# Two pieces of side work joined into one with two strands, late weights awaited one by one, and corrected durations in a planner

## The chip, the cores and the metric

The kernel runs on one core of a Trainium2 chip. The core has a matrix engine (PE, with its weight load shown apart as PEld), a vector engine (DVE), an activation engine (ACT), GpSimd (POOL), and SyncE (SP), which here issues nearly all DMA transfers. The metric is the device time of one execution in microseconds. The kernel before took 860.47, 861.98 and 862.07 us in three runs, a median of 861.98 us. The execution that the profiler recorded took 859.36 us, of which its span is 857.6 us.

## The reference, cut to what matters

One transformer block over 2048 tokens of width 512 in bfloat16: attention with 32 heads of size 16, then a gated feed-forward part (hidden width 1792), each behind a layer norm whose scale and shift come from a small vector `c`.

```python
sa, ca, ga, sb, cb, gb = split(silu(c) @ w_mod)
h = layernorm(x) * (1 + ca) + sa
q, k, v = split_heads(h @ wqkv)                      # 32 heads of 16
x = x + ga * (softmax(q @ k.T / 4) @ v) @ wo
h = layernorm(x) * (1 + cb) + sb
x = x + gb * (gelu(h @ w_gate) * (h @ w_up)) @ w_down
```

The scores are 32 x 2048 x 2048 numbers, and each of them needs an exponential.

## The kernel before

The tokens are cut into six sets (`SETS`): three of 512 queries (sets 0, 1, 2), one of 256 (set 3) and two of 128 (sets 4, 5). Each set is gone through in eight units `qd` of four heads. A unit consists of rounds; a round is four tiles of scores of 128 x 512, one for each head. All in all there are 2048 tiles, and a place in this order is called a position; `ends[k]` is the position at which set k's scores are finished (`ends[2]` = 1536, `ends[3]` = 1792, `ends[4]` = 1984, the last is 2048).

**The main line of work.** PE computes two or three tiles of scores into PSUM (`ps_sc`), ACT turns them into exponentials `E` (line 327, one instruction for 1024 or 1536 columns), and PE multiplies them with the values into `ps_pv` (line 314). For some rounds, which I call vector rounds, DVE takes the place of ACT: four instructions of 512 columns each (`dreg<-ps_sc` or `mreg<-ps_sc`, line 339) make an approximate exponential, and four more of 2048 columns (`mreg<-dreg`, `mreg<-mreg`) make shifted copies. PE then multiplies five versions instead of one with the values. A vector round takes four tiles off ACT and puts eight instructions on DVE. While one is being filled, each group has two tiles for ACT and one for DVE.

**The side work.** Everything else runs as generators that hand PE one matmul at a time, in the order of a list made by `plan`: the projections of the first layer, and for each finished set k the output projection `side_wo(k)` (needs the normalized attention outputs `onorm` of all eight units), the second layer norm as a chain of small DVE tasks, and `side_ffn(k)`: transposes, then gate products `G` and up products `U` for 14 blocks of 128 hidden columns, then the down projection. All side matmuls go through one PSUM bank, `ps_mi`. Only the first generator of the list is asked; while it waits for something (`until`), no side work is done at all.

**Who sets the order.** The instruction streams are written out by a planner when the kernel is built. It goes through the work with its own model of durations (`model` and `cost`) and always issues what it believes can start next. Each entry of `plan` has a first position and a due position; the columns that remain, divided by the positions up to the due one, earn credit. Side work advances when there is credit. From `ends[2]` on, a vector round is begun only while the credit is under 2048 (of at most 4096) or while side work waits for `onorm` or `osb`. In other words, side work behind its schedule keeps vector rounds from being begun.

**The late weights.** For sets 0 to 2 the feed-forward weights are streamed from memory into staging buffers. For sets 3 to 5 they stay in SBUF: ten parts of 256 KB are loaded early, and eleven late ones (seven of `w_up`, one of `w_gate`, three of `w_down`) go into places that the down projection of set 2 uses to its end. They are issued one per two positions after `("ffn", 2)` is done, and `side_ffn(3)` begins with a wait for `"weights"`, which is set after the last of them has been issued. After that, `scale_down` multiplies the down weights by `gb` on DVE.

**Set 3's second layer norm** writes into `tb2`, the front of `hreg`; the products `prodT` that set 2's down projection reads lie in the same place.

At the end, `near_end` computes the last normalizations of set 4 on PE, `side_wo(4)` follows, then the first part of set 4's feed-forward work; the tail finishes sets 4 and 5 after the last exponential.

Of the kernel before, what the change touches and what calls it, by code (L numbers as in the profile page):

```python
# [13 lines left out]
P = 128  # L14
# [65 lines left out]
class _Recorder:  # L80
# [166 lines left out]
    def model(self, op, t, cost):  # L247
# [6 lines left out]
        elif eng == "pe":  # L254
# [3 lines left out]
            if mode != self.pe_mode:  # L258
                t = max(t, self.pe_end + 105)
# [6 lines left out]
            end = t + max(cols, 64) / 2.4  # L266
# [20 lines left out]
    def cost(self, eng, out, ins, kind):  # L287
        n = 1
        for _, k in (out if kind != "bn" else ins[0]).ap[1:]:
            n *= int(k)  # L290
        aps = [out] + list(ins)
        ps = any(self.kind.get(a.tensor.name) == "ps" for a in aps)
        small = all(mybir.dt.size(a.dtype) == 2 for a in aps)
        if eng == "act":
            return n * 0.833 + (57 if ps else 92)
        if eng == "pool":
            return n * 3.0 + 100
        f = 1
        if not ps:
            f = {("ts", True): 4, ("ts", False): 2, ("tt", True): 2}.get((kind, small), 1)  # L300
        elif small:
            f = 1.4
        return n * 1.042 / f + 68
# [116 lines left out]
class _Kernel(_Recorder):  # L420
# [12 lines left out]
    def alloc(self):  # L433
# [9 lines left out]
        self.tb2 = hreg[:, 0:4 * D].rearrange("p (t n) -> p t n", t=4)  # L443
        wreg = sb("wreg", [P, NDC * 1536], BF16)
# [407 lines left out]
    def weight_parts(self):  # L852
# [9 lines left out]
        return g[:6] + d[:4], u + g[6:] + d[4:]  # L862
# [23 lines left out]
    def normed(self, k, i):  # L886
        return self.E[:, NSL - 1, :] if k == len(SETS) - 1 else self.tb2[:, i, :]
# [75 lines left out]

    def side_wo(self, gi):
# [4 lines left out]
        for i in range(n):  # L969
            for g in self.merged(gi):  # L970
# [11 lines left out]
    def side_ffn(self, gi, part=None):  # L982
# [28 lines left out]
        else:  # L1011
            yield from self.until("weights")
# [14 lines left out]
        def G(ci):  # L1027
# [3 lines left out]
            load(0, ci + 1)  # L1031
            for b0 in range(0, m, kpb):
# [10 lines left out]
        def U(ci):  # L1043
# [4 lines left out]
            load(1, ci + 1)  # L1048
            for b0 in range(0, m, kpb):
# [28 lines left out]
        if part is not None:  # L1078
# [4 lines left out]
            return  # L1083
        if not flow:
# [59 lines left out]
    def plan(self, ends, nsplit):  # L1144
# [15 lines left out]
        due = (ends[1] + 30, ends[2] + 30, ends[3] + 30, ends[4] - 20)  # L1160
        for k, e in enumerate(due):
            s0 = ends[k] + 33
            w.append((lambda k=k: self.side_wo(k), s0, min(e, s0 + 15 * SETS[k][1] // P)))
            w.append((lambda k=k: self.side_ffn(k), s0, e))
        k, s0 = len(SETS) - 2, ends[-2] - 16
        w.append((lambda: self.near_end(k, 6, self.mi[:, 0:P]), s0, s0))
        w.append((lambda: self.near_end(k, 7, self.mi[:, 0:P]), s0, s0))
        w.append((lambda: self.side_wo(k), s0, s0))
# [49 lines left out]
    def stream(self):  # L1218
# [140 lines left out]
        while cg <= group[units[-1]]:  # L1359
            parts = early or late  # L1360
            if parts and pos >= loaded and (pos >= ends[2] + 8 if early else ("ffn", 2) in self.have):
                parts.pop(0)()
# [426 lines left out]
```

## Time and profile before

| what | us |
|---|---|
| three runs | 860.47, 861.98, 862.07 |
| the profiled execution, its span | 859.36, 857.6 |
| ACT busy in the span | 830.9 (97%) |
| PE busy | 788.0 (92%) |
| DVE busy | 705.6 (82%) |
| exponentials on ACT | 698 instructions, 803.2 |
| last exponential of the main line ends | 836.1 |

Busy time is a sum over stages. Up to 836 us ACT works on exponentials nearly without a gap; from there to the end a chain over all engines finishes the last 256 tokens. The attention outputs of set 3's eight units leave PSUM between 625.05 and 722.44 us and are normalized (`onorm<-osb,rb`) between 642.35 and 736.92 us; sets 4 and 5 follow. The granted PE clock was full in all slices but the first and the last moments.

### The profile page before, as it was taken

To read this page: it belongs to the slowest core of one execution; us is meant where nothing else is said; L and a number is where in the kernel's file an instruction comes from. 1 tells how busy PE (TensorE), PEld (TensorE's weight loads), DVE (VectorE), ACT (ScalarE), POOL (GpSimd) and SP (SyncE) were. 2 spreads that over 40 slices of the span, in tenths; PEclk is the share of its full clock that TensorE was granted. 3 is DMA by queue.
4 is the path that set the end of the run, shared out by engine and by line. 5 is a ranking of instruction groups with operands and counts; after the bars stand their busy time and mean duration, and the time that the engine had idled before them with its cause. 6 is when DMAs were issued, how large, how long until landed. Compare 5 with 4: busy or idle time off the path is not lost.

```text
span 857.6 us, 27732 instructions
## 1 busy us (share of the span) xinstructions
PE 788.0 (92%) x12443; PEld 285.8 (33%) x12445; DVE 705.6 (82%) x1363; ACT 830.9 (97%) x747; POOL 4.5 (1%) x12
## 2 busy tenths in 40 slices
PE   8899998999999998999999899999998999988987
PEld 3333332322222222222222222222343333435556
DVE  7855989787999898999899999988887877477664
ACT  7999999999999999999999999999999999999992
POOL 1000000000000000000000000000000000000000
PEclk9999999999999999999999999999999999999999
DMA  9000000000002112110003102110233222150000
GB/s 313 27 15 17 5 10 11 10 13 9 8 9 78 47 37 57 55 37 21 12 18 91 49 21 60 37 55 12 59 97 116 57 70 56 33 144 11 20 7 14
DMA packets 66169, 38.97 MB, mean 45 GB/s; under 512 B 18657, under 2 KB 63906, under 8 KB 66050
## 3 DMA queue, kind: packets, MB, share of 16 engines
q1 hardware_dynamic: 65520, 36.67, 15.3%
q8 instruction: 97, 1.59, 0.8%
q10 hardware_dynamic: 530, 0.53, 0.2%
q14 instruction: 22, 0.18, 0.1%
HBM read 33.81 MB, written 2.61 MB: 42 GB/s over the span
## 4 chain that ended last, share of the span: by engine, by line
ACT 72%; PE 13%; DVE 8%; DMA 4%; SPq 2%; issue 1%; DVEq 0%
ACT E L327 69%; PE ps_mi L314 6%; PE ps_sc L314 5%; PE ps_pv L314 2%; ACT wreg L327 2%; DMA rb<-scr_rec 2%; SPq L377 2%; DVE st L367 1%; DVE mreg L339 1%; DMA den<-scr_den 1%; DMA scr_rec<-rden 1%; DVE dreg L339 1%; DVE wreg L344 1%; DVE hreg L339 1%; DVE nwt L331 0%
## 5 line engine op out<-in xcount | busy, mean ns | idle before, releaser
L327 ACT ACTIVATE E<-ps_sc 128x1536 bf16<-128x1536 f32 (+2 forms) x698 | 803.2, 1344 | 13.7 <-PE ps_sc L314 13.1
L314 PE MATMUL ps_sc<-qT,kmo 32*128 32x512 bf16 (+2 forms) x1408 | 182.7, 323 | 10.8 <-ACT E L327 8.7
L314 PE MATMUL ps_sc<-qT,kme 32*128 32x512 bf16 (+2 forms) x1408 | 176.1, 323 | 15.7 <-ACT E L327 13.0
L314 PE MATMUL ps_pv<-E,vaug 128*17 128x512 bf16 (+2 forms) x2396 | 171.3, 319 | 4.7 <-DVE osb L348 2.3
L339 DVE TENSOR_SCALAR dreg<-ps_sc 128x512 uint16<-128x512 f32 x200 | 137.7, 690 | 36.5 <-PE ps_sc L314 33.6
L339 DVE TENSOR_SCALAR mreg<-dreg 128x2048 uint16<-128x2048 uint16 x200 | 131.5, 682 | 1.7 <-PE ps_pv L314 1.5
L314 PE MATMUL ps_mi<-wreg,mreg 128*32 128x512 bf16 (+2 forms) x1504 | 110.5, 370 | 11.6 <-DVE wreg L344 7.3
L314 PE MATMUL ps_pv<-mreg,vs 128*17 128x512 bf16 (+2 forms) x1424 | 103.7, 344 | 1.9 <-DVE mreg L339 1.4
L314 PEld LDWEIGHTS ps_sc<-qT,kme 32*128 32x128 bf16 x1408 | 49.0, 91 | 135.2 <-ACT E L327 103.6
L314 PEld LDWEIGHTS ps_sc<-qT,kmo 32*128 32x128 bf16 x1408 | 49.5, 91 | 121.2 <-ACT E L327 93.7
L314 PEld LDWEIGHTS ps_pv<-E,vaug 128*17 128x17 bf16 x2396 | 53.0, 89 | 90.5 <-issue 61.1
L339 DVE TENSOR_SCALAR mreg<-ps_sc 128x512 uint16<-128x512 f32 x96 | 66.2, 690 | 19.5 <-PE ps_sc L314 18.6
L339 DVE TENSOR_SCALAR mreg<-mreg 128x2048 uint16<-128x2048 uint16 x96 | 63.3, 686 | 0.9 <-PE ps_pv L314 0.9
L314 PEld LDWEIGHTS ps_mi<-wreg,mreg 128*32 128x32 bf16 (+1 forms) x1504 | 34.4, 95 | 61.4 <-issue 21.1
L314 PEld LDWEIGHTS ps_pv<-mreg,vs 128*17 128x17 bf16 x1424 | 32.3, 89 | 35.8 <-DVE mreg L339 16.6
L348 DVE CAST wreg<-ps_mi 128x512 bf16<-128x512 f32 x51 | 35.0, 686 | 10.7 <-PE ps_mi L314 10.1
L344 DVE SCALAR_TENSOR_TENSOR wreg<-wreg,ps_mi 128x512 bf16<-128x512 bf16 x51 | 34.9, 685 | 10.3 <-ACT wreg L327 6.7
L314 PE MATMUL ps_mi<-hreg,wreg 128*32 128x512 bf16 (+1 forms) x496 | 40.0, 377 | 1.9 <-DVE hreg L339 1.0
L331 DVE TENSOR_TENSOR wreg<-wreg 128x1024 bf16<-128x1024 bf16 (+1 forms) x60 | 35.6, 604 | 0.6
L314 PE MATMUL ps_mi<-mreg,hreg 128*32 128x512 bf16 x384 | 32.7, 384 | 0.0
L327 ACT ACTIVATE wreg<-wreg 128x1024 bf16<-128x1024 bf16 (+1 forms) x30 | 30.4, 1023 | 0.0
L331 DVE TENSOR_TENSOR onorm<-osb,rb 128x512 bf16<-128x512 f32 (+2 forms) x44 | 23.7, 540 | 7.4 <-DMA rb<-scr_rec 7.3
(149 smaller groups left out, 558.3 us busy)
## 6 DMA issues: line engine op xcount, KB each, us to landing
mreg<-in_B_w_up_dram SPq DMA_DIRECT2D x25, 256.0 KB, 3.1
mreg<-in_B_w_gate_dram SPq DMA_DIRECT2D x21, 256.0 KB, 3.0
rb<-scr_rec SPq DMA_DIRECT2D x96, 32.0 KB, 1.8
mreg<-in_B_w_down_dram SPq DMA_DIRECT2D x12, 256.0 KB, 2.7
dreg<-in_B_w_down_dram SPq DMA_DIRECT2D x9, 256.0 KB, 4.3
mreg<-in_w_mod_dram SPq DMA_DIRECT2D x1, 2048.0 KB, 12.7
out_dram<-xs SPq DMA_DIRECT2D x15, 128.0 KB, 1.7
xs<-in_A_x_dram SPq DMA_DIRECT2D x3, 512.0 KB, 6.5
```

The source lines that it names most:

```text
L314: return self.rec("pe", lambda e: e.matmul(out, lhsT, rhs, start=start, stop=stop, tile_position=tp), [lhsT, rhs], [out], cost=(n, int(rhs ...
L327: return self.rec("act", lambda e: e.activation(out, in_, func, scale=scale, **kw), rd, wr, cost=self.cost("act", out, [in_], "act"))
L331: return self.rec(eng, lambda e: e.tensor_tensor(out, a, b, op), [a, b], [out], cost=self.cost(eng, out, [a, b], "tt"))
L339: return self.rec(eng, lambda e: e.tensor_scalar(out, a, s1, s2, **kw), rd, [out], cost=self.cost(eng, out, [a], "ts") + (60 if len(rd) > ...
L344: return self.rec("dve", lambda e: e.scalar_tensor_tensor(out, a, s, b, op0=op0, op1=op1), rd, [out], cost=self.cost("dve", out, [a, b], " ...
L348: return self.rec(eng, lambda e: e.tensor_copy(out, in_), [in_], [out], cost=self.cost(eng, out, [in_], "ts"))
L367: return self.rec("dve", lambda e: e.bn_stats(out, in_), [in_], [out], cost=self.cost("dve", out, [in_], "bn"))
L377: return e.dma_start(out, in_)
```

## The change

Four things are changed.

1. *Durations of the planner's model.* An ACT instruction on PSUM is priced 6 ns lower; a PE matmul is given 12 columns (when four small ones run side by side) or 6 columns more; a change of PE's tile mode 3 ns less; the statistics instruction of the layer norm 95 ns more on DVE. No instruction's work changes by this, but the order can.
2. *Late weights.* The wait for all of them at the head of `side_ffn` becomes a wait in front of each product that needs one: part 6 of `w_gate` from block 12 on, and the part of `w_up` that a `U` uses.
3. *Two strands.* The down projection leaves `side_ffn` and becomes `side_down`. For sets 0 and 1 it still follows at once. Set 2's down projection is joined with set 3's output projection by `mix(a, b)`, and set 3's down projection with `near_end` and set 4's output projection. `mix` offers the second strand first; where that one waits and no tile of it is half done in the bank, one whole tile of the first strand is done. An output projection from set 3 on begins only when all eight units are there. Due positions change to fit.
4. *A place of their own* (`tb3`, behind `prodT`) for the second layer norms of sets 3 and 4.

```diff
-                t = max(t, self.pe_end + 105)
+                t = max(t, self.pe_end + 102)
...
-            end = t + max(cols, 64) / 2.4
+            end = t + max(cols + (12 if mode else 6), 64) / 2.4
...
-            return n * 0.833 + (57 if ps else 92)
+            return n * 0.833 + (51 if ps else 92)
...
-        return n * 1.042 / f + 68
+        return n * 1.042 / f + 68 + (95 if kind == "bn" else 0)
...
+        self.tb3 = hreg[:, NFC * 512:NFC * 512 + 2 * D].rearrange("p (t n) -> p t n", t=2)
...
-        return self.E[:, NSL - 1, :] if k == len(SETS) - 1 else self.tb2[:, i, :]
+        return self.E[:, NSL - 1, :] if k == len(SETS) - 1 else (self.tb2 if k < 3 else self.tb3)[:, i, :]
...
+    def mix(self, a, b):
+
+        if self.dry:
+            yield from a
+            yield from b
+            return
+        inside = over = False
+        while True:
+            x = next(b, 0)
+            if x == 0:
+                yield from a
+                return
+            if x is not None or inside or over:
+                inside = x is not END and (inside or x is not None)
+                yield x
+                continue
+            while True:
+                y = next(a, 0)
+                over = y == 0
+                if over:
+                    break
+                yield y
+                if y is END:
+                    break
...
     def side_wo(self, gi):
...
         for i in range(n):
+            if gi >= 3:
+                for qd in range(8):
+                    yield from self.until(("onorm", gi, qd))
...
-        else:
-            yield from self.until("weights")
...
+            if not flow and fcs[-1] >= 12:
+                yield from self.until(("wg", 6))
...
+            if not flow:
+                yield from self.until(("wu", fcs[-1] // 2))
...
+        if gi < 2:
+            yield from self.side_down(gi)
+
+    def side_down(self, gi):
...
-        due = (ends[1] + 30, ends[2] + 30, ends[3] + 30, ends[4] - 20)
+        due = (ends[1] + 30, ends[2] + 30, ends[3] + 0, ends[4] - 40)
         for k, e in enumerate(due):
             s0 = ends[k] + 33
-            w.append((lambda k=k: self.side_wo(k), s0, min(e, s0 + 15 * SETS[k][1] // P)))
-            w.append((lambda k=k: self.side_ffn(k), s0, e))
+            if k < 3:
+                w.append((lambda k=k: self.side_wo(k), s0, min(e, s0 + 15 * SETS[k][1] // P)))
+            w.append((lambda k=k: self.side_ffn(k), 0 if k == 3 else s0, e))
+            if k == 2:
+                w.append((lambda: self.mix(self.side_down(2), self.side_wo(3)), 0, ends[3] + 30))
         k, s0 = len(SETS) - 2, ends[-2] - 16
-        w.append((lambda: self.near_end(k, 6, self.mi[:, 0:P]), s0, s0))
-        w.append((lambda: self.near_end(k, 7, self.mi[:, 0:P]), s0, s0))
-        w.append((lambda: self.side_wo(k), s0, s0))
+
+        def last():
+            yield from self.near_end(k, 6, self.mi[:, 0:P])
+            yield from self.near_end(k, 7, self.mi[:, 0:P])
+            yield from self.side_wo(k)
+        w.append((lambda: self.mix(self.side_down(3), last()), 0, ends[4] + 0))
...
-                parts.pop(0)()
+                key, f = parts.pop(0)
+                f()
+                self.done(key)
```

## The prediction

> **What bounds the kernel now.** I first read the page's busy times, then the stretches of the last third, then the order in time on SP, PE and DVE around the place that the change touches, and last the groups by form in two stretches, to get a rate of exchange.
>
> ```profile
> PE 788.0 (92%) x12443; PEld 285.8 (33%) x12445; DVE 705.6 (82%) x1363; ACT 830.9 (97%) x747; POOL 4.5 (1%) x12
> ...
> 550.00:650.00 100.00, 95.41 (x1462) 32.87 (x1462) 89.41 (x160) 99.98 (x91) 0.00 (x0) 1.00 0.19 52
> 650.00:753.00 103.00, 95.23 (x1786) 38.48 (x1778) 69.99 (x127) 101.62 (x83) 0.00 (x0) 1.00 0.26 73
> 753.00:764.00 11.00, 9.08 (x174) 3.37 (x174) 8.96 (x30) 11.00 (x9) 0.00 (x0) 1.00 0.75 218
> 764.00:808.00 44.00, 39.91 (x1171) 24.12 (x1162) 31.96 (x71) 43.48 (x40) 0.00 (x0) 1.00 0.06 13
> 808.00:836.00 28.00, 24.99 (x770) 16.27 (x770) 18.20 (x48) 27.21 (x22) 0.00 (x0) 1.00 0.06 12
> 836.00:857.60 21.60, 16.92 (x244) 13.87 (x238) 10.35 (x27) 6.04 (x12) 0.00 (x0) 1.00 0.05 14
> ```
>
> The stretches give the span's part and then busy time of PE, PEld, DVE, ACT and POOL, the granted clock and the DMA share. ACT is the bound: from 650 to 836 us it is idle for 186 - 183.31 = 2.7 us. So time is won by taking tiles off ACT (more vector rounds), by a shorter tail (21.6 us), or hardly at all. DVE, which makes the vector rounds, is 89% busy from 550 to 650 but 68% from 650 to 753 and 73% from 764 to 808: room that is not used.
>
> Next, around 735 to 764 us (start, duration, instruction):
>
> ```profile
> 736.92 0.41 DVE L331 TENSOR_TENSOR onorm<-osb,rb 128x256 bf16<-128x256 f32 x1
> ...
> 741.35 0.69 DVE L331 TENSOR_TENSOR wreg<-ps_mi,gb 128x512 bf16<-128x512 f32 x1 [2.81 <-PE ps_mi L314]
> ...
> 747.66 0.69 DVE L331 TENSOR_TENSOR wreg<-ps_mi,gb 128x512 bf16<-128x512 f32 x1 [5.04 <-PE ps_mi L314]
> ...
> 752.76 0.39 PE L314 MATMUL ps_mi<-wo,onorm 128*32 128x512 bf16 x4
> ...
> 761.09 0.40 PE L318 MATMUL ps_mi<-ident,hreg 128*128 128x128 bf16 x4
> ...
> 749.24 2.59 SPq L377 DMA_DIRECT2D mreg<-in_B_w_up_dram  x3
> ...
> 758.96 0.47 SPq L377 DMA_DIRECT2D hreg<-in_B_w_down_dram  x1
> ```
>
> The reader sees set 3's last `onorm` ready at 736.92, while set 2's down projection goes on to its fourth eviction at 747.66; only then comes set 3's output projection (to 753.15), its norm chain, and the wait for the late weights, whose last is issued at 758.96. The next side matmul, a transpose, is at 761.09. For 7.9 us there is no side work. Forty filler matmuls stand there instead (24 into `ps_sc`, 16 into `ps_mi`), ten groups of 0.22 us, and PE is idle for 11 - 9.08 = 1.9 us. ACT doesn't mind: it is busy 11.00 of 11.00.
>
> **The change part by part.**
>
> *Set 3's output projection between down tiles.* At 736.92 the third down tile is in the bank; after its eviction (741.35) two output tiles fit in. It is the same work in another order: two tiles of 20 matmuls, five groups of 0.22 us each, and two evictions of 0.69, about 4.5 us with the attention matmuls between (752.76 + 0.39 - 748.5 before). Set 2's last down eviction goes from 747.7 to about 752. The norm chain of set 3 (753.9 to 757.2 before: statistics, eight steps of 0.2, two normalizations of 0.4) falls under that last tile, where DVE waited 5.04 us; so it costs nothing while the tile lasts, and some 3 us if that cover is missed. `tb3` makes this legal, since the tile still reads the front of `hreg`; it adds no instruction. The wait for all eight units costs nothing, since the last was 10 us early.
>
> *Late weights.* Eleven DMAs stay, issued after set 2's last tile, so about 4 us later than now. What waits on SP behind them is the chain of a unit's denominators (`scr_den`, `den`, `scr_rec`, `rb`), as it does now. Transposes and the first gates need early weights only and go at about 753 instead of 761.1. The first `U` needs part 0 of `w_up`: it comes after two gate pieces, some 4 us later, and these transfers land 4.3 us after issue. Issue at 752.5, landing at 757, first `U` at 757 to 758: hidden, or up to 2 us of waiting, with PE's score matmuls queued behind it and ACT behind those. Later parts come one per 1.34 us, and a pair of `G` and `U` takes over 4 us, so they are early. `scale_down` (14 of 0.34 us on DVE) moves 4 us later and still ends 20 us before set 3's down projection needs it (793.8).
>
> *What the side work gains* is the 7.9 us hole. How it turns into ACT time is seen from two stretches (count, then busy):
>
> ```profile
> L339 DVE TENSOR_SCALAR dreg<-ps_sc 128x512 uint16<-128x512 f32 x32 | 22.1, 691 | 6.3 <-PE ps_sc L314 5.7
> L339 DVE TENSOR_SCALAR mreg<-ps_sc 128x512 uint16<-128x512 f32 x14 | 9.7, 691 | 1.9 <-PE ps_sc L314 1.8
> ...
> L339 DVE TENSOR_SCALAR mreg<-ps_sc 128x512 uint16<-128x512 f32 x8 | 5.5, 692 | 5.0 <-PE ps_sc L314 5.0
> L339 DVE TENSOR_SCALAR dreg<-ps_sc 128x512 uint16<-128x512 f32 x8 | 5.5, 691 | 3.9 <-PE ps_sc L314 3.6
> ...
> 715.69 35.91 ACT L327 ACTIVATE E<-ps_sc 128x1536 bf16<-128x1536 f32 x29
> 752.22 16.23 ACT L327 ACTIVATE E<-ps_sc 128x1536 bf16<-128x1536 f32 x12 [0.61 <-PE ps_sc L314]
> ```
>
> The first pair (550 to 650) is 46 tiles, 11.5 vector rounds in 100 us, beside 400 side matmuls (128 + 96 + 96 + 80) or 100 groups. The second pair (650 to 753) is 4 rounds in 103 us beside 712 side matmuls, 178 groups. So 78 groups were paid with 7.5 rounds: 10.4 groups for one. The hole, at 178/103 = 1.73 groups per us, is 13.7 groups, or 1.3 rounds. From the other side, DVE bounds it: a round costs 4 x 0.61 + 2.5 = 4.9 us there (four copies ran in 2.50), and DVE is idle for 12.0 us from 764 to 808, room for 2.4 rounds. Rounds are whole; I take 2, between the two, and keep 1 and 3 for the range.
>
> *Price of a round.* Twelve instructions in a row took 16.23 us; without the last one's 0.2 of overhang that is 1.335 for three tiles. In the 29 of the other row eight have two tiles: (35.7 - 21 x 1.335)/8 = 0.96. Four groups with a vector round take 4 x 0.96 instead of 4 x 1.335, so 1.5 us are saved; by tiles alone it would be 4 x 0.445 = 1.78. I take 1.65. Two rounds: 3.3 us.
>
> *Due positions.* Set 2's gates and ups are now due at 1792 and its down tiles at 1822, before all of it at 1822: nearly the same pace. Set 3's gates and ups are due at 1944 and its down tiles at 1984, before both at 1964; starting earlier, they are less pressed. Cost between one round lost and one won, 1.65 us either way; I take 0.
>
> *Durations.* Only the order can change. The ACT price falls towards the measured one (512 x 3 x 0.833 + 51 = 1.331 against 1.335 above), PE's rises to 218 ns for 512 columns (rows: 0.22 a group). In the main line ACT is idle too little for a better order to bring more than the 2.7 us above; a worse order costs what it uncovers. Per vector round the nearest scale is again 1.65 us. I take 0, between one round more and two fewer.
>
> *Tail.* It starts with the last exponential. Set 4's output projection hangs on its last unit (its matmuls start at 812.78, right after the `onorm` of 812.76), not on side work. 0.
>
> Sum against the profiled execution: 859.36 - 3.3 = 856.1. The runs' median of 861.98 is 2.6 above that execution, so a median of 858.7 us is forecast.
>
> **The rivals.**
>
> *B, the hole is filled and nothing follows.* The side work is early, but rounds aren't begun: those before the hole are limited by the same gate, products and norm chains, and after it few candidate rounds remain. Then only ACT's own gaps at this place count, the 0.61 us at 752: 861.4. For it: in the 11 us without side work there was no vector round at all, although DVE had 2 us left. Against it: the last two rounds before 808 came just as the side work caught up. The Trainium skill has a rule that would give this result (Perfetto Trace Analysis, Optimization Strategy: look for the gaps on the most contended engine and remove what causes them); that ACT is that engine the trace agrees, at 97%, and by the rule alone a hole on PE under a full ACT is worth nothing.
>
> *C, slower: vector rounds are lost to the planner's dearer PE.* Place: sets 3 to 5, where matmuls are narrow. 12 columns are 2.3% of 512 but 4.7% of 256 and 9.4% of 128. PE is really busy 92% there; a planner that sees it as full lets fewer side matmuls go ahead of scores, credit stays over its bound, and rounds aren't begun. It decides once two of the six rounds after 650 us go (16 + 8 tiles in the rows before 808) while the hole brings none: 861.98 + 3.3 = 865.3. For it: PE has only 4 us idle in 764 to 808. Against it: the side work itself has 8 us more.
>
> *D, a new wait.* The first `U` finds its weights late and holds up scores behind it: up to 2 us, and the norm chain of set 3 misses its cover, 3 us of side work (half a round, 0.8): 861.98 + 2.0 + 0.8 = 864.8 without any round won. For it: DMA share is 0.75 there. Against it: landing in 4.3 us even so.
>
> **How the numbers follow.** The forecast has 0.57, on its own 855.5 to 860.3 (four rounds of 1.6, or one). B has 0.22, C 0.14, D 0.07. Under 0.2% (1.7 us) a measurement of this kernel can hardly tell a change from none. Faster by more: the forecast's 0.57. Within it: B, and a milder D, 0.24. Slower: C and the rest of D, 0.19. The range goes down to four rounds of 1.78, 854.9, and up to 864.5, short of C's full price.
>
> **What the profile after would show.** Right: set 3's output projection (`ps_mi<-wo,onorm`) before the last of set 2's down tiles; its transposes within 2 us after that tile, and no fillers there; at least four and up to twelve more tiles in `uint16<-128x512` after 650 us and as many fewer for ACT; the last exponential before 833 us; the tail still 21 to 22 us. Wrong: the same number of such tiles or fewer, ACT idle over 3 us from 650 on, or a PE wait on the `w_up` transfers. A gain or loss of rounds before 600 us would come from the durations alone.

## The result, and the profile after

The changed kernel takes 863.65 us (median of nine runs, 862.43 to 866.18), the kernel before beside it 861.98 (nine runs, 858.12 to 862.66). The ratio on record is 1.004, 95% interval [1.0024, 1.0056] (the quotient of the two medians, 1.0019, is smaller): slower, where faster was forecast. The time lies in the forecast's range; the sign is wrong. The profiled execution took 864.27 us, its span is 862.5, which is 4.9 more than before.

The profile's busy times of the changed kernel:

```profile
PE 795.4 (92%) x12358; PEld 288.6 (33%) x12360; DVE 701.4 (81%) x1355; ACT 831.8 (96%) x747; POOL 4.5 (1%) x12
```

ACT is busy 0.9 us longer (831.8 against 830.9) and idle 4.0 us longer (862.5 - 831.8 = 30.7 against 857.6 - 830.9 = 26.7). So in these two executions four fifths of the difference is time in which the bounding engine stood still. The stretches say where (columns as in the prediction: the stretch, its length, busy PE, PEld, DVE, ACT, POOL, granted clock, DMA share, GB/s); the last two rows look closer at two places.

```profile
550.00:650.00 100.00, 95.37 (x1425) 32.44 (x1425) 88.72 (x155) 99.70 (x90) 0.00 (x0) 1.00 0.18 48
650.00:753.00 103.00, 95.25 (x1815) 39.03 (x1808) 77.75 (x151) 102.29 (x86) 0.00 (x0) 1.00 0.25 69
753.00:764.00 11.00, 10.91 (x188) 4.28 (x189) 8.62 (x15) 11.00 (x11) 0.00 (x0) 1.00 0.07 20
764.00:808.00 44.00, 36.44 (x1130) 24.39 (x1130) 31.61 (x77) 41.36 (x36) 0.00 (x0) 0.96 0.30 79
808.00:840.50 32.50, 28.65 (x738) 15.92 (x738) 14.55 (x41) 29.59 (x23) 0.00 (x0) 0.95 0.06 14
840.50:862.50 22.00, 19.01 (x253) 15.33 (x252) 12.43 (x31) 6.46 (x13) 0.00 (x0) 1.00 0.05 14
...
782.00:785.00 3.00, 3.00 (x84) 2.02 (x88) 2.27 (x6) 1.72 (x2) 0.00 (x0) 0.61 0.43 130
811.00:814.00 3.00, 3.00 (x70) 1.52 (x65) 0.00 (x0) 2.08 (x2) 0.00 (x0) 0.60 0.02 5
```

The hole is gone: PE is busy 10.91 of the 11 us from 753 to 764, where it was 9.08. But from 764 on ACT is idle for 2.64 + 2.91 = 5.55 us, against 0.52 + 0.79 = 1.31 before. The tail is 22.0 against 21.6. New is also the granted clock: twice, from 782.7 and from 810.0 us, PE had half its clock for a stretch of 3.41 us; before, the clock stayed full in these stretches.

Next the order around the change, PE's side matmuls first (the last line is set 3's first gate in the kernel before), then DVE's evictions:

```profile
737.72 1.03 PE L314 MATMUL ps_mi<-wo,onorm 128*32 128x512 bf16 x16
741.73 0.40 PE L314 MATMUL ps_mi<-wo,onorm 128*32 128x512 bf16 x4
...
763.92 0.40 PE L314 MATMUL ps_mi<-mreg,hreg 128*32 128x512 bf16 x4
765.35 0.40 PE L318 MATMUL ps_mi<-ident,hreg 128*128 128x128 bf16 x4
...
768.83 0.95 PE L314 MATMUL ps_mi<-wreg,qT 128*32 128x256 bf16 x28
...
763.67 1.06 PE L314 MATMUL ps_mi<-wreg,qT 128*32 128x256 bf16 x32
```

```profile
742.18 0.69 DVE L331 TENSOR_TENSOR xs<-xs,ps_mi 128x512 bf16<-128x512 bf16 x1 [0.61 <-PE ps_mi L314]
748.05 0.69 DVE L331 TENSOR_TENSOR wreg<-ps_mi,gb 128x512 bf16<-128x512 f32 x1 [1.88 <-PE ps_mi L314]
...
756.64 0.69 DVE L331 TENSOR_TENSOR wreg<-ps_mi,gb 128x512 bf16<-128x512 f32 x1 [0.43 <-PE ps_mi L314]
...
764.38 0.69 DVE L331 TENSOR_TENSOR wreg<-ps_mi,gb 128x512 bf16<-128x512 f32 x1 [0.45 <-PE ps_mi L314]
```

Set 3's output projection lies between down tiles, as it should, and the transposes follow the last down tile in 1.0 us. But that tile is evicted at 764.38 instead of 747.66, and set 3's first gate starts at 768.83 instead of 763.67: the side work has no hole any more and is 5.2 us later all the same.

The groups of score tiles that DVE makes, from 650 to 753 us and from 753 to the last exponential, say what it was spent on:

```profile
L339 DVE TENSOR_SCALAR dreg<-ps_sc 128x512 uint16<-128x512 f32 x15 | 10.4, 690 | 6.1 <-PE ps_sc L314 6.1
L339 DVE TENSOR_SCALAR mreg<-ps_sc 128x512 uint16<-128x512 f32 x6 | 4.2, 692 | 2.8 <-PE ps_sc L314 2.8
...
L339 DVE TENSOR_SCALAR dreg<-ps_sc 128x512 uint16<-128x512 f32 x4 | 2.8, 692 | 0.8 <-PE ps_sc L314 0.8
L339 DVE TENSOR_SCALAR mreg<-ps_sc 128x512 uint16<-128x512 f32 x2 | 1.4, 692 | 0.5 <-PE ps_sc L314 0.5
```

That is 21 tiles (the first begun at 649.5) and 6, where there were 16 and 8. Counted at other bounds: 262 tiles up to 640 us (271 before), 30 from 640 to 764 (17), none after 764 (8): 73 rounds for 74. So rounds were made earlier, beside set 2's side work, and that side work ends later.

How ACT came to stand still at 781 us, in the order of time on SP, then on DVE, PE and ACT. (`rb` holds the reciprocal denominators that `onorm` needs; they are written to memory as `scr_rec` and read back spread out.)

```profile
772.01 0.34 SPq L377 DMA_DIRECT2D scr_rec<-rden  x1
772.39 0.43 SPq L377 DMA_DIRECT2D dreg<-in_B_w_up_dram  x1
772.87 0.51 SPq L377 DMA_DIRECT2D hreg<-in_B_w_gate_dram  x1
773.48 1.67 SPq L377 DMA_DIRECT2D xs<-in_B_w_down_dram  x1
777.03 2.51 SPq L377 DMA_DIRECT2D rb<-scr_rec  x4
```

```profile
780.89 0.43 DVE L331 TENSOR_TENSOR onorm<-osb,rb 128x256 bf16<-128x256 f32 x1 [2.25 <-DMA rb<-scr_rec]
781.24 0.68 DVE L344 SCALAR_TENSOR_TENSOR wreg<-wreg,ps_mi 128x512 bf16<-128x512 bf16 x1
...
781.97 1.05 PE L314 MATMUL ps_mi<-wreg,qT 128*32 128x256 bf16 x28 [2.65 <-DVE wreg L344]
...
783.28 0.63 ACT L327 ACTIVATE wreg<-wreg 128x512 bf16<-128x512 bf16 x1 [1.73 <-DVE wreg L331]
...
787.05 1.45 ACT L327 ACTIVATE E<-ps_sc 128x1536 bf16<-128x1536 f32 x1 [0.47 <-PE ps_sc L314]
...
788.91 5.48 ACT L327 ACTIVATE E<-ps_sc 128x1536 bf16<-128x1536 f32 x4 [0.41 <-PE ps_sc L314]
```

`rb` of a unit of sets 4 and 5 is issued 5.0 us after `scr_rec`, amid the burst of late weights (in the kernel before 3.7 us for the unit that met the burst there, and 1.4 to 3.2 for those after 765 us). DVE reaches the `onorm` that needs it and waits 2.25 us; behind that instruction stands the eviction that frees `ps_mi`; behind that eviction stands a side matmul, and behind it on PE the scores. ACT loses 1.73, at an activation whose input (`wreg`, L331) stands behind the same `onorm` on DVE; the scores are there only just after it, at 783.56. It loses another 0.47 and 0.41 in the 3 us after the stretch at half the clock, which ends at 786.1. The second place has the same form with another wait in front, and no late weight near (the last was issued at 780.66):

```profile
808.02 0.29 DVE L331 TENSOR_TENSOR onorm<-osb,rb 128x128 bf16<-128x128 f32 x1 [2.13 <-DMA rb<-scr_rec]
808.23 0.95 DVE L351 RECIPROCAL rb<-ps_mi 128x128 f32<-128x128 f32 x1
...
809.24 0.83 PE L314 MATMUL ps_mi<-xs,hreg 128*32 128x512 bf16 x12 [2.80 <-DVE rb L351]
...
810.65 1.45 ACT L327 ACTIVATE E<-ps_sc 128x1536 bf16<-128x1536 f32 x1 [1.99 <-PE ps_sc L314]
813.03 4.13 ACT L327 ACTIVATE E<-ps_sc 128x1536 bf16<-128x1536 f32 x3 [0.92 <-PE ps_sc L314]
```

Here `near_end` of set 4 has put its small product into `ps_mi` and DVE must read it; DVE waits for `rb` of another unit; set 3's down projection, whose first matmul is the one at 809.24, can't begin.

### The profile page after: what moved, and what is told of

It reads as the page before. It is cut to its first block, busy times and chain, and to the rows that moved or that the text cites. A ratio compares the mean times of both kernels' runs of the same rounds, so it can differ in the third digit from the quotient of the medians.

```text
span 862.5 us, 27550 instructions
## 1 busy us (share of the span) xinstructions
PE 795.4 (92%) x12358; PEld 288.6 (33%) x12360; DVE 701.4 (81%) x1355; ACT 831.8 (96%) x747; POOL 4.5 (1%) x12
## 4 chain that ended last, share of the span: by engine, by line
ACT 82%; PE 10%; DMA 3%; DVE 2%; SPq 1%; issue 1%; DVEq 0%
ACT E L327 80%; PE ps_sc L314 4%; PE ps_mi L314 3%; ACT wreg L327 2%; PE ps_pv L314 2%; SPq L377 1%; DMA scr_rec<-rden 1%; DMA mreg<-in_w_mod_dram 1%; DMA rb<-scr_rec 1%; DMA den<-scr_den 1%; DMA mreg<-in_B_w_gate_dram 0%; DVE dreg L339 0%; DVE wreg L344 0%; DVE st L367 0%; DVE nwt L331 0%
## 5 line engine op out<-in xcount | busy, mean ns | idle before, releaser
L314 PE MATMUL ps_sc<-qT,kme 32*128 32x512 bf16 (+2 forms) x1408 | 177.9, 325 | 16.1 <-ACT E L327 13.2
L314 PE MATMUL ps_pv<-E,vaug 128*17 128x512 bf16 (+2 forms) x2412 | 173.7, 320 | 4.8 <-DVE osb L348 1.7
L339 DVE TENSOR_SCALAR dreg<-ps_sc 128x512 uint16<-128x512 f32 x196 | 135.4, 691 | 44.3 <-PE ps_sc L314 42.3
L339 DVE TENSOR_SCALAR mreg<-dreg 128x2048 uint16<-128x2048 uint16 x196 | 128.3, 684 | 0.7 <-PE ps_pv L314 0.6
L314 PE MATMUL ps_mi<-wreg,mreg 128*32 128x512 bf16 (+2 forms) x1504 | 112.9, 372 | 7.5 <-DVE wreg L344 4.8
L314 PE MATMUL ps_pv<-mreg,vs 128*17 128x512 bf16 (+1 forms) x1360 | 102.0, 350 | 0.8 <-DVE mreg L339 0.3
L314 PEld LDWEIGHTS ps_pv<-E,vaug 128*17 128x17 bf16 x2412 | 55.0, 90 | 94.9 <-issue 64.1
L331 DVE TENSOR_TENSOR wreg<-wreg 128x1024 bf16<-128x1024 bf16 (+1 forms) x60 | 35.8, 602 | 0.5
L348 DVE COPY osb<-ps_pv 128x512 f32<-128x512 f32 (+2 forms) x43 | 23.1, 537 | 12.0 <-PE ps_pv L314 11.6
```

Of the source, the lines that this page charges most:

```text
L314: return self.rec("pe", lambda e: e.matmul(out, lhsT, rhs, start=start, stop=stop, tile_position=tp), [lhsT, rhs], [out], cost=(n, int(rhs ...
L331: return self.rec(eng, lambda e: e.tensor_tensor(out, a, b, op), [a, b], [out], cost=self.cost(eng, out, [a, b], "tt"))
L339: return self.rec(eng, lambda e: e.tensor_scalar(out, a, s1, s2, **kw), rd, [out], cost=self.cost(eng, out, [a], "ts") + (60 if len(rd) > ...
L348: return self.rec(eng, lambda e: e.tensor_copy(out, in_), [in_], [out], cost=self.cost(eng, out, [in_], "ts"))
```

## The experiments

Theories: *rounds* (the number of vector rounds, moved by the corrected durations, decides); *lane* (the side work is one lane, done in a fixed order; the due positions let rounds delay set 2's part of it, so that the gain is spent before it comes); *stalls* (late DMAs, DVE waiting in order, PE behind it, then the half clock); *end* (the join of set 3's down projection with set 4's output projection makes the end later). Each kernel ran 12 times, in three groups of four beside 35 runs of the kernel before, whose median was 860.68, 862.11 and 863.46 us in the three; so ratios are compared, not times; they differ from the quotients of the medians by up to 0.0021. The row "after" is the nine runs of the result. "Half" is the mean number of half-clock stretches in one run, from its mean granted clock (one of 3.41 us lowers that by 0.002).

ACT's idle time is that from 640 us to the last exponential, in the profiled execution; those of 1, 7 and 12 hold a longer half-clock stretch (10 or 14 us) that begins ahead of 470 us, which the medians don't share, and the profiled executions of 1, 7, 8, 11 and 12 took 3 to 5 us more than the median of their kernel. One execution's idle time is a rough measure: DVE, ACT and SP do the same instructions in the same order in the kernel before and in kernel 3 up to 757 us, and ACT is idle for 1.4 us from 640 to 757 in one and for 4.4 in the other; kernels 2 and 6 are the same up to 821 us, with 6.9 and 4.2 from 640 to there.

| kernel | ratio [95%] | rounds | ACT busy | ACT idle | half |
|---|---|---|---|---|---|
| before | 1 | 74 | 830.9 | 2.7 | 0.9 to 1.3 |
| after | 1.0040 [1.0024, 1.0056] | 73 | 831.8 | 6.3 | 1.8 |
| 1 durations alone | 1.0009 [0.9992, 1.0026] | 72 | 834.6 | 1.6 | 0.8 |
| 2 all but durations | 1.0032 [1.0013, 1.0051] | 76 | 828.1 | 7.6 | 1.9 |
| 3 piecewise waits alone | 1.0016 [0.9998, 1.0033] | 75 | 829.4 | 6.3 | 1.8 |
| 4 after, late weights spread | 1.0011 [0.9994, 1.0029] | 74 | 830.6 | 2.8 | 0.7 |
| 5 after, set 4 first | 1.0048 [1.0028, 1.0068] | 73 | 831.8 | 7.3 | 2.4 |
| 6 as 5, old durations | 1.0017 [0.9999, 1.0036] | 75 | 829.3 | 5.4 | 2.2 |
| 7 after, set 2 due 20 earlier | 0.9996 [0.9979, 1.0013] | 73 | 832.3 | 4.6 | 1.3 |
| 8 as 2, set 2 due 30 earlier | 0.9970 [0.9949, 0.9991] | 75 | 829.2 | 5.4 | 1.8 |
| 9 before, set 2 due 30 earlier | 1.0037 [1.0017, 1.0056] | 73 | 834.0 | 6.0 | 2.3 |
| 10 as 8, late weights spread | 1.0012 [0.9998, 1.0027] | 75 | 829.1 | 7.1 | 2.6 |
| 11 as 3, set 2 due 30 earlier | 1.0005 [0.9985, 1.0026] | 75 | 829.8 | 9.1 | 1.5 |
| 12 after, both repairs (4 and 7) | 0.9984 [0.9964, 1.0004] | 72 | 834.2 | 1.3 | 1.0 |

**1 and 2: durations alone, and all but the durations.** Kernel 1 is the kernel before with the four `+` lines, kernel 2 the changed kernel with the four `-` lines.

```diff
-                t = max(t, self.pe_end + 105)
+                t = max(t, self.pe_end + 102)
...
-            end = t + max(cols, 64) / 2.4
+            end = t + max(cols + (12 if mode else 6), 64) / 2.4
...
-            return n * 0.833 + (57 if ps else 92)
+            return n * 0.833 + (51 if ps else 92)
...
-        return n * 1.042 / f + 68
+        return n * 1.042 / f + 68 + (95 if kind == "bn" else 0)
```

> The kernel before with part 1 of the change alone (corrected durations). The program has 72 vector rounds instead of 74. Theory R (rounds): the corrected durations lose vector rounds all along the main line, because in the planner's model ACT now goes through a position faster and DVE slower; each lost round costs 1.65 us. It expects 2 x 1.65 = 3.3 us more than before, ratio 1.003 to 1.005, with ACT idle from 650 us to the last exponential of the main line about as before (2.7 us). Theory S (stalls): the loss of the changed kernel is made by its new order of side work between 764 and 816 us, where ACT is idle for 5 us; durations alone do nothing to it, so within 0.2% of before.

> The changed kernel with the old durations (parts 2, 3 and 4 alone). The program has 76 vector rounds. Theory R: two rounds more than before, 3.3 us less, ratio 0.995 to 0.998. Theory S: the late transfers again fall beside set 3's gates, DVE waits in order for a normalization behind them, and set 4's normalizations stand between down tiles; ACT idle from 764 us to the last exponential is 5 to 6 us instead of 1.3, so 3.3 us won and some 4 us lost, ratio 0.999 to 1.003. Theory T (tail): set 4's output projection ends 12 us later than before, as in the changed kernel, and what is left of its feed-forward work makes the tail over 23 us.

The durations alone cost two rounds (72) and no time that can be told from none; all the rest with the old durations has two rounds more (76) and is 0.32% slower. There ACT is idle for 5.0 us from 764 us on and the tail is 25.8 us, as the theories of stalls and of the end expected. The theory of rounds falls: 72 rounds run as fast as 74, and 76 are slower than both. A round does have its price, in ACT's work: from 76 to 72 rounds ACT's busy time rises from 828.1 to 834.4 us (mean of kernels 1 and 12), 1.6 a round, against 1.65 forecast. What is gained there comes back as idle time.

**3: the piecewise waits alone**, on the kernel before.

```diff
-        else:
-            yield from self.until("weights")
...
+            if not flow and fcs[-1] >= 12:
+                yield from self.until(("wg", 6))
...
+            if not flow:
+                yield from self.until(("wu", fcs[-1] // 2))
```

> The kernel before with part 2 alone: late weights awaited piece by piece, down projection and output projections in their old order and places, old durations and due positions. The program has 75 vector rounds. Transposes of set 3 can start when its norm is done (about 758 us instead of 761). Theory R: one round more, 1.65 us less, ratio 0.997 to 0.999. Theory S: the gates now run beside the transfers, DVE waits for a normalization as in the changed kernel, ACT idle at 764 to 790 us 2 us or more; ratio 0.999 to 1.002.

The time is hardly to be told from that of before (1.0016). One round more, but 6.3 us of idle ACT, 3.28 of it in one gap at 659.3 us, long before any late weight. The instructions and their order are those of the kernel before up to 757 us, so this gap is not the edit's: `den<-scr_den`, a step of the denominators' chain, landed 5.6 us after its issue here and 4.3 there. The wait of DVE, before and in kernel 3:

```profile
656.26 0.20 DVE L351 RECIPROCAL rden<-den 128x8 f32<-128x8 f32 x1 [2.10 <-DMA den<-scr_den]
...
659.26 0.20 DVE L351 RECIPROCAL rden<-den 128x8 f32<-128x8 f32 x1 [3.46 <-DMA den<-scr_den]
```

Kernels 8 and 11, whose order is still that of before at this place, have the same gap (2.86 and 3.19 us).

**4: the changed kernel with the late weights one per six positions.**

```diff
-                loaded = pos + (8 if early else 2)
+                loaded = pos + (8 if early else 6)
```

> The changed kernel with one number different: a late weight part every 6 positions instead of every 2, which spreads the eleven transfers over three times the time. The order is the same until then; 74 vector rounds instead of 73. Theory S: the normalization at 780.9 us is no longer late, PE's gap of 2.65 us there and ACT's idle 1.7 us go, and so does the clock's drop to half behind it: 2.5 us less than the changed kernel by that and 1.65 by the round, so 859 to 860.5, ratio to before 0.997 to 0.999. Theory R: only the round counts, 862.0, ratio 1.000, and ACT idle from 764 us on stays over 4 us.

ACT's idle time falls from 6.3 to 2.8 us and the half-clock stretches from 1.8 to 0.7 a run, with the lane as late as in the changed kernel (set 2's last down matmul at 764.7 us against 763.9). The ratio falls from 1.0040 to 1.0011. So stalls carry a part of the loss. How much is not clear: one round more (74) is worth up to 0.0019 of the 0.0029 by the price above, and the expected 0.997 to 0.999 was not reached. The trace suggests why not. The main line's last exponential ends at 835.5 us instead of 840.5, but the span falls only from 862.5 to 861.4, since the tail is 25.9 us: set 4's output projection is evicted at 825.9, nearly as late as in the changed kernel (826.9). In kernels 2, 4 and the changed one the span ends 35.0 to 35.6 us after that eviction, in the others 37.4 us or more; so in these three the end seems to hang on set 4, not on the main line, and that is a place where a late lane can cost time. The burst as the stalls' cause is less well borne out: the wait at the first place is still there (DVE waits 1.82 us for `rb` at 780.41, and ACT is idle for 0.63 and 0.87 behind it); the second is the one that is gone, and there no late weight had been in the way. Kernel 5, whose order is that of the changed kernel up to 824 us, shows both of its stalls again (ACT idle for 2.83 us at 785.8 and 1.42 at 813.6), so they belong to that order.

**5 and 6: set 4's output projection ahead of the rest of set 3's down projection**, once set 4's last unit has left PSUM; 6 has the old durations as well.

```diff
-            if x is not None or inside or over:
+            if x is not None or inside or over or (hold is not None and hold in self.have):
...
-        w.append((lambda: self.mix(self.side_down(3), last()), 0, ends[4] + 0))
+        w.append((lambda: self.mix(self.side_down(3), last(), ("osb", k, 7)), 0, ends[4] + 0))
```

> The changed kernel, but from the moment set 4's last unit has left PSUM the second strand is not interrupted by a down tile any more. The order is the same until then. Theory W (two ends): the kernel ends at the later of two things, 21 us after the last unit leaves PSUM (841.1 in the changed kernel) and 35.4 us after set 4's output projection is evicted (826.9); the structure makes the second late, since a wait of 1 us for a normalization is filled with a down tile of 6 to 8 us. Set 4's eviction comes 5 to 8 us earlier (819 to 822), the remaining down tile fills the wait of the norm chain, and the end is bound by the first thing: 0 to 1.5 us less than the changed kernel. Theory M (main line only): set 4's output projection is off the path; no change at all. Theory S: same ACT idle of 4 us from 764 to 816 us as in the changed kernel, ratio to before 1.002 to 1.004.

> The same hold, with the old durations: 75 vector rounds (76 in the structure alone). Theory W: in the structure alone the main line ended its last unit at 838.7, which would allow an end at 859.7, but set 4's eviction at 828.6 made it 863.7. With the hold the eviction comes 6 to 8 us earlier and the last unit's exit decides: 3 us less than the structure alone, ratio to before 0.997 to 1.000. Theory M: one round fewer than the structure alone, 1.65 us more than it, ratio 1.004 to 1.006.

In 5 set 4's last eviction comes at 823.0 instead of 826.9 us, and the time doesn't improve (1.0048). In 6 the tail does fall, from 25.8 us in kernel 2 to 22.0, and the ratio from 1.0032 to 1.0017, with overlapping intervals. In 5 the main line itself ended later (842.9 for 840.5 us), so that the earlier eviction could gain nothing. The join at the end is at most a small part of the changed kernel's loss; it seems to decide where the main line is early, as in 2 and 4.

**7 and 8: set 2's gates and ups due earlier**, by 20 positions in the changed kernel (7), and by 30 with the old durations and the edit of 5 (8). With this due position that edit changes nothing: the instructions and their order are the same without it, so 8 is kernel 2 with one number changed.

```diff
-        due = (ends[1] + 30, ends[2] + 30, ends[3] + 0, ends[4] - 40)
+        due = (ends[1] + 30, ends[2] + 30, ends[3] - 20, ends[4] - 40)
```

> The changed kernel with one number different: set 2's gates and ups are due 20 positions earlier (1772). 73 vector rounds as there, but seven of the 30 tiles from 640 to 764 us move behind 764. Theory L (lane): set 3's gates started 5 us later than before because vector rounds begun in set 2's stage slowed its side work by 16 us, and everything behind inherits that. Here set 2's last down tile ends at 750 to 754 instead of 764, set 3's gates start before 760, set 4's eviction is 3 to 5 us earlier, and the time is 1 to 2 us less than the changed kernel, ratio 1.001 to 1.003. Theory R: same number of rounds, same time, ratio 1.003 to 1.005.

> The prediction's case made real: the change with old durations, with the hold, and with set 2's gates and ups due 30 positions earlier, so that the hole is filled: set 3's gates should start at 756 to 758 instead of 763.7. 75 vector rounds, one more than before. Theory of the prediction: the lane's gain becomes rounds, 1.65 us less than before, ratio 0.997 to 0.999. Theory S: with the hole filled PE has less to spare in 753 to 764, transfers of late weights stand beside gates, ACT idle from 764 us on is 4 us or more, and more clock windows fall; ratio 1.000 to 1.003. Theory W: with the last unit out by 836 and set 4's eviction by 820, an end at 857, ratio 0.998 to 1.000.

In 7 set 2's last down matmul comes at 758.0 us instead of 763.9 (750 to 754 was expected), set 3's first gate at 762.9 (before 760 was expected), and the loss is gone (0.9996), more than the 1.001 to 1.003 of the theory. In 8 the last down matmul comes at 745.3, and the kernel is faster than before, 0.997 [0.9949, 0.9991], median 858.41 us. Seven of its runs took 857.4 to 858.6 us with a granted clock of 0.998 or 1, five 862.2 to 864.8 with 0.990 to 0.996; the profiled one is of the five. From 764 us on ACT is idle for only 1.0 us in it, where the theory of stalls expected 4. The order in time on PE in kernel 8:

```profile
745.01 0.61 PE L314 MATMUL ps_mi<-mreg,hreg 128*32 128x512 bf16 x8
746.55 0.82 PE L314 MATMUL ps_mi<-wo,onorm 128*32 128x512 bf16 x12
...
756.03 0.66 PE L318 MATMUL ps_mi<-ident,hreg 128*128 128x128 bf16 x4 [0.36 <-DVE hreg L339]
...
758.83 1.06 PE L314 MATMUL ps_mi<-wreg,qT 128*32 128x256 bf16 x32 [0.17 <-DVE wreg L339]
```

Set 3's output projection stands behind all of set 2's down tiles, as before the change; `mix` had nothing to mix. What is earlier is the gate: 758.83 against 763.67 us. The due position brings 2.8 us of that (760.9 in kernel 9, which still waits for all late weights); the rest fits the piecewise waits, since the last late weight is issued only at 763.02. Both kernels go the way that the theory of the lane says; 7 gains more than it.

**9: the kernel before with set 2's side work due 30 positions earlier.**

```diff
-        due = (ends[1] + 30, ends[2] + 30, ends[3] + 30, ends[4] - 20)
+        due = (ends[1] + 30, ends[2] + 30, ends[3] + 0, ends[4] - 20)
```

> The kernel before with one number changed: set 2's side work is due 30 positions earlier. Question: is the gain of the early variant (0.997) that of the due position alone, or of set 3's gates no longer waiting for all late weights? Due position alone: set 2's last down matmul at 743 to 746 us and a ratio of 0.996 to 0.998. The gates' wait: set 2's down tiles end as early, but the first gate of set 3 stays at 759 us or later, since the late weights are waited for as one block, ACT stands 3 us or less from 640 us on as before, and the ratio is 0.999 to 1.002.

Neither answer: set 2's last down matmul comes at 744.9 us and the kernel is slower, 1.0037. One round is lost, and ACT is idle for 6.0 us. An early lane is no gain of its own.

**10: kernel 8 with the late weights spread** as in 4.

> The early variant (structure of the change, old durations, set 2's gates and ups 30 positions earlier; without the hold, which changes no instruction there), and the late weights one per 6 positions instead of one per 2. Theory of stalls: the burst's DMAs hold up the denominators' chain, DVE and PE behind it; spread out, ACT's idle time from 640 us on falls from 5.35 to under 3.5 us, the half-clock windows from 1.75 to under 1.2 per run, and the ratio is 0.994 to 0.997, under the early variant's. Rival (the place of the lane alone): 0.9965 to 0.999, whatever the windows do.

Outside both: 1.0012, half-clock stretches 2.6, ACT's idle time 7.1 us. Its DVE and PE at the largest gap:

```profile
807.77 0.29 DVE L331 TENSOR_TENSOR onorm<-osb,rb 128x128 bf16<-128x128 f32 x1 [2.19 <-DMA rb<-scr_rec]
...
809.59 0.83 PE L314 MATMUL ps_mi<-xs,hreg 128*32 128x512 bf16 x12 [2.80 <-DVE rb L351]
```

The second stall of the changed kernel, nearly word for word, and the last late weight was issued at 775.81 us, 27 us before this `rb`. So the burst is not needed for it; what both share is the order: an `onorm` set ahead of an instruction that frees `ps_mi`, some 2 us before its `rb` lands. In kernel 4, where this stall is gone, the product of `near_end` is read ahead of the `onorm`.

**11: piecewise waits and the early due position on the kernel before, without strands.** It is kernel 3 with the diff of 9.

> The kernel before with the piecewise waits for late weights and set 2's due position 30 earlier, without any strands and with the old durations. If the gain of the early variant is that of an early lane with piecewise waits, and the strands give nothing at set 2 (there set 3's output projection stands behind the down tiles all the same): first gate of set 3 before 761 us, ratio 0.996 to 0.9985. If the strands are needed: 0.9995 to 1.002, as with the piecewise waits alone (1.0016).

1.0005, with set 3's first gate at 762.1 us (before 761 was expected): closer to what was expected if strands are needed, but the intervals of 8 and 11 overlap. ACT is idle for 9.1 us here, 3.2 of them at 659.4, before the edits change any order, so the comparison doesn't isolate the strands.

**12: the changed kernel, durations and all, with the edits of 4 and 7.**

> The changed kernel, all of it, with both repairs: set 2's gates and ups due 20 positions earlier, late weights one per 6 positions. If the two causes add (each repair alone took 0.3 to 0.4% of the time off): last down matmul of set 2 at 758 us or earlier, ACT idle from 640 us under 3.5 us, ratio 0.996 to 0.9985. If they are one cause seen twice, or rounds count after all (72 planned against 74 before): 0.9995 to 1.002, as each alone.

0.9984, from 1.0040: at the upper edge of what was expected if the two add. The sum of their gains would give 0.9967, and the interval, up to 1.0004, covers the other answer too, so it isn't decided. With kernel 1 it has the fewest rounds, 72, and it has the least idle time, 1.3 us. Its stretches:

```profile
764.00:808.00 44.00, 38.94 (x1174) 23.22 (x1172) 36.62 (x85) 44.00 (x41) 0.00 (x0) 1.00 0.24 65
808.00:842.50 34.50, 32.07 (x854) 18.32 (x847) 16.87 (x46) 34.48 (x28) 0.00 (x0) 1.00 0.07 15
```

ACT is idle for 0.02 us in 78.5, where the changed kernel left 5.55 in the same place. DVE's waits for `rb` are still there, and one of them, 2.68 us, is longer than the one at 808 in the changed kernel, but in this order ACT has work left behind them:

```profile
809.18 0.29 DVE L331 TENSOR_TENSOR onorm<-osb,rb 128x128 bf16<-128x128 f32 x1 [0.97 <-DMA rb<-scr_rec]
812.15 0.29 DVE L331 TENSOR_TENSOR onorm<-osb,rb 128x128 bf16<-128x128 f32 x1 [2.68 <-DMA rb<-scr_rec]
```

## Why the prediction was wrong

In the profiled executions the sum stood for a span of 857.6 - 3.3 = 854.3 us; it was 862.5. Of the 8.2 us between, 4.2 are ACT's busy time (831.8 for 830.9 - 3.3 = 827.6: one round lost instead of two won) and 4.0 its idle time. So two things failed: the rounds that the filled hole was to buy, and the idle time that the sum let stand.

**Set 3's output projection between down tiles: right in itself.** It ran from 737.72 to 742.1 us, its second tile was evicted at 742.18, and the norm chain ended under the next down tile. No filler matmuls are left there.

**Set 2's last eviction at 752: the step that failed, through "Due positions ... I take 0".** It came at 764.38. 4.5 us of the delay are the output projection, as forecast; the other 12 go with rounds. 3.25 more of them were made between 640 and 764 us (30 tiles for 17); by the prediction's own rate of 10.4 groups for a round that is 34 groups, at 1.73 a microsecond 20 us of side work, more than what was seen. Neither part of the change does so by itself: the durations alone make 20 tiles in that stretch (kernel 1), the rest alone 21 (kernel 2), both together 30, more than 3 and 4 over the 17 make; so two steps that the prediction each took as 0 work on each other here. The prediction had the rate in hand and used it in one direction alone: a hole buys rounds. It did not ask where the planner would buy, and it took the two due positions as nearly the old pace. Moving set 2's forward by 20 positions takes that stretch back to 20 tiles and the loss away (kernel 7); by 30, with the old durations, to 17 tiles, and the kernel is faster (kernel 8). And of the rounds made early some were missing late: no tile after 764 us, where eight had been. That the rounds beside set 2 are what made its side work late is well borne out by this; that the lateness is what cost the time is not, since kernel 4 has the same 30 tiles and the same late lane at 1.0011, and kernel 9 has an early lane at 1.0037.

**Late weights: right for the first `U`, wrong for the chain.** The first `U` did not wait. But "What waits on SP behind them is the chain of a unit's denominators, as it does now" passed over this: the burst now met another unit's chain, at a place where DVE had an eviction and PE a gate behind the waiting `onorm`. That, and the same wait at 808, is rival D's mechanism, a new wait that holds up scores, at another transfer than the one named; D had a chance of 0.07 and a price of 864.8.

**Price of a round: right as ACT work, wrong as time.** 1.6 us of ACT's busy time were measured, 1.65 forecast; but the sum let ACT's idle time stand at 2.7 us. It ran from 1.3 to 9.1 over these kernels, a spread larger than the whole forecast gain; some 3 us of such a spread came between executions of one and the same order. The Trainium skill (Perfetto Trace Analysis, Optimization Strategy) would look for the gaps on the most contended engine and at what they wait for; that rule, which stood with rival B, fits the 5.55 us of gaps better than the count of rounds did.

**Durations, 0 with one round more to two fewer: right taken alone**, at the range's edge: two fewer in kernel 1, and a ratio of 1.0009. Rival C's rounds were lost, but up to 640 us (260 tiles for 271), not in sets 3 to 5, and they cost nothing that could be measured. **Tail, 0: right by luck** (22.0 against 21.6 in the changed kernel; 20.6 to 25.9 over the experiments). Its reason failed: set 4's output projection no longer follows its last unit's `onorm` at once, but waits 6 us behind a down tile of set 3, and is evicted at 826.9 instead of 814.8 us. The tail seems to have stayed short only because the main line was late as well.

```profile
818.69 0.29 DVE L331 TENSOR_TENSOR onorm<-osb,rb 128x128 bf16<-128x128 f32 x1
...
824.94 1.05 PE L314 MATMUL ps_mi<-wo,onorm 128*32 128x512 bf16 x16
```

Of the signs that the prediction named for being right, four came true (output projection ahead of the last down tile, transposes within 2 us of it, no fillers, a tail of 22.0 us) and two did not (27 tiles after 650 us for 24, under the four more that were asked; the last exponential at 840.5, not before 833). Of the three that were to prove it wrong one came: ACT idle for over 3 us from 650 on.

What stays open: how the 0.4% divides between the late lane, the stalls and the late set 4; how much of kernel 8's 0.3% is due to the strands (at set 3's down projection and set 4's output projection they do act); and which orders bring an `onorm` ahead of its `rb`. Each edit also moved such waits at places behind it that it didn't aim at, and the waits differ between executions of one order, so differences of 0.2% between two of these kernels shouldn't be put down to the edit's meaning.

## What to carry to other kernels

Where side work and an optional relief of the bounding engine draw on the same slack, a hole that is filled is spent where the planner's due position lets it be spent: work out the moved stage's new finishing time with the relief priced in, not only what the hole would buy. Before counting saved work on an engine that is 97% busy, list what could make it idle: follow each small DMA's consumer, what stands behind that consumer in order on its engine, and who waits for that. In a kernel whose order is written by a model, judge an edit by several orders, since a microsecond or more of waiting moves with any of them, and profile one order more than once before a gap in it is put down to an edit. Where two paths end close together, as the main line and set 4's work do here, a repair of one gains no more than the other allows.

## What the runs showed of the hardware

In the changed kernel a pause of 2.65 and one of 2.80 us on PE were each followed, within 0.8 us of its end, by a stretch of 3.41 us at half the granted clock. The Trainium skill (TensorE: Matmul & The Clock Gate, Part 1) gives a window of 3413 ns, and half the clock after an idle window; the length agrees, but the pauses seen here were shorter than the window. The pause alone doesn't decide it: kernel 6 has pauses of 2.45 and 2.28 us without such a stretch behind them, and in kernels 1 and 12 a stretch of 13.65 us begins at 461.9 and 461.4 us with no pause of PE over 1.5 us anywhere in the main line. Longer stretches were 6.83, 10.24 or 13.65 us, two, three and four times 3.41.

Fitted over the runs of each kernel, a stretch of 3.41 us went with 0.87 to 1.76 us more time, a quarter to a half of its length, in a kernel that ACT bounds. The fit holds the pause that came with it as well, so this is not the price of the clock alone. Part of it may come behind the stall itself: ACT was idle for another 0.47, 0.41 and 0.92 us after the two pauses.

A small transfer of the denominators' chain (`den<-scr_den`) landed 4.3, 5.6, 5.9 and 6.0 us after its issue at the same place of the same order (the kernel before, 3, 11 and 8).
